# DVE's 32x32 block transposes for softmax sums, the spreading of their reciprocals and the maxima, in place of TensorE products

## The chip, the cores and the metric

The kernel runs on one core of a Trainium2 chip. The metric is device time in microseconds of one execution; 0.2% of it (2.6 us) is about what can be told from no change. Engines are named as the profile does: PE (TensorE; PEld its weight loads), DVE (VectorE), ACT (ScalarE), POOL (GpSimd), SP (the queue that issues nearly all DMAs).

## The reference

Two independent layers over 2048 positions and 448 channels, concatenated. Half A is an S4D convolution: a kernel `K` made of exponentials of 256 modes per channel, an FFT convolution with `u`, and a skip term. Half B is multi-head attention with 16 heads of width 28; the part that matters here:

```python
scores = jnp.einsum("bhqd,bhkd->bhqk", q, k) * scale
p = _softmax(scores, axis=-1)
o = jnp.einsum("bhqk,bhkd->bhqd", p, v)
return (lambda x, *d: x.transpose(*d))(o, 0, 2, 1, 3).reshape(B, S, D) @ wo
```

## The kernel before

All work is recorded through a wrapper (`Kept`, line 77), so nearly every instruction has line 77 in the profile and is told by its tiles. In a first part (about 225 us: projections of q, k, v and the start of half A) a scheduler is free to order each engine's instructions (`KEPT["p"]` is empty). From `nc.kept = KEPT["a"]` on, every engine runs in the order in which the code calls it.

**The main loop** has 256 steps (line 1061 on): 16 units (4 head groups of 4 heads times 4 blocks of 512 queries), 16 steps each, one step per 128 keys. `ORDER` (line 35) is a step's order: four score products `s0` to `s3` (tile `pss`, then an exponential on ACT into `p`), four products `m0` to `m3` for the row maxima of the unit that comes next (tile `pm`; `m0` is followed by a Relu on ACT into `rl`, `m1` by a fused add-and-maximum on DVE, custom instruction `rl<-pm,rl`; `m2` and `m3` by a DVE reduction `mx<-pm`), `pv` (the product with v of the step before, tile `po`), two places `f` for a piece of half A or of the output projection (`slot`, line 1012), and three places `v` for one DVE instruction of half A's powers (`g`, `zg`). POOL computes other powers (`e`, `eu`) all the while. The maxima run 19 steps ahead of their use (`sm = s + NK + LEAD`).

All `pm` tiles (maxima, pieces, and the products described next) take turns in a ring of three PSUM buffers (`w_tile`, line 127): a product waits until the third tile before it has been read.

**At a unit's end** (`fin`, line 789) ACT copies the finished `po` to SBUF as `o`: for each head 28 rows of output, and in row 28 of its 32 the softmax sum, because v carries a column of ones. Then, as pieces that take a place `f` each two and four places later (`UG`, `soon_slot`):
- `sums`: PE products `sel,o` pick the sums, queries on partitions; DVE takes their reciprocals `r` from PSUM; ACT spreads each over 32 columns into `rb`.
- `scale`: PE products `ident,rb` turn `rb` back into the layout of `o`; DVE multiplies `on = o * pm`, the second operand in PSUM. `on` goes to DRAM or, in the last head group, to four output projections `project` (products `ua,og` and `ua,on`).

**At the end of a unit's maxima** `max_join` (line 210) joins three maxima per row (`m`, 128x16), and two places later `max_end` (line 214) has PE transpose `m` to 16x128 in PSUM (`ident,m`), from which DVE makes minus the maximum as a high and a low part (`mh`, two instructions from PSUM); two DMAs put them into two rows of `qhat`, so that the score product subtracts the maximum. The score products of that unit begin three steps after the join.

The other PE pieces: `e,g` and `w,ko` (56 blocks of half A's kernel, done at about step 198), `ua,w` and `ua,mt` (transform of u, 64 pieces, to about step 101), `yk,mw`, `p,mw` and `zi,wb` (spectrum and inverse transform, from step 192 on).

Of the kernel before, what the change touches and what calls it, by code (L numbers as in the profile page):

```python
# [8 lines left out]
F32 = mybir.dt.float32  # L9
# [83 lines left out]
def body(ctx, tc, a, out):  # L93
# [26 lines left out]
    sel = const.tile([128, HG], F32, name="sel")  # L120
    kones = const.tile([128, 1], F32, name="kones")
    w1 = const.tile([128, 2, 128], F32, name="w1")

# [87 lines left out]
        m_u[u, 1] = q_p.tile([128, HG * 4], F32, name="m1", bufs=2)  # L211
        nc.vector.tensor_reduce(m_u[u, 1], m_u[u].rearrange("p a b c -> p (a b) c")[:, :, :n], axis=AX.X, op=ALU.max)

    def max_end(u, ps):
        nc.tensor.transpose(ps[:16, :128], m_u[u, 1], ident)
        mh = q_p.tile([16, 2, 128], F32R, name="mh")
        nc.vector.tensor_scalar(mh[:, 0, :], ps[:16, :128], -1.0, None, op0=ALU.mult)
        nc.vector.scalar_tensor_tensor(mh[:, 1, :], ps[:16, :128], -1.0, mh[:, 0, :].bitcast(F32),
                                       op0=ALU.mult, op1=ALU.subtract)
        mh_u[u] = mh  # L220

    def max_put(u, queue=nc.sync):
        for i in range(2):
            queue.dma_start(q_u[u][4 * (DH + i):4 * (DH + i) + 1, :, :].rearrange("p h (t q) -> p (h t) q", t=4).bitcast(F32),
                                mh_u[u][:, i, :].bitcast(F32))


    with ExitStack() as st:
        sst, xst, wst = ExitStack(), ExitStack(), ExitStack()
# [91 lines left out]
        nc.sync.dma_start(sel, a["sel"])  # L321
        nc.sync.dma_start(w1, a["w1"])
        def split_w(s):
            for k in range(NCK):
# [276 lines left out]
        nc.scalar.activation(half_pi[:1], half_pi[:1], AF.Exp)  # L601
        n_st.close()
        max_join(0, 2)
        max_end(0, ps_t.tile([128, CQ], F32, name="pt"))
        max_put(0, nc.scalar)
        sst.close()


# [180 lines left out]
    def fin(u, s_):  # L789
        g, c = divmod(u, NQ)  # L790
        o = kq_p.tile([128, CQ], F32, name="o")
        nc.scalar.activation(o, o_u[u], AF.Copy)
        on = kq_p.tile([128, CQ], F32, name="on", bufs=2)
        rb = kq_p.tile([128, 4, HG, 32], F32, name="rb")
        og = og_u.pop(u, None)

        def sums():
            pw = w_tile()
            for t in range(4):
                mm32(pw[:, t * HG:(t + 1) * HG], o[:, t * 128:(t + 1) * 128], sel, start=True, stop=True)  # L800
            r = kq_p.tile([128, 4, HG], F32, name="r", bufs=2)
            nc.vector.reciprocal(r, pw[:, :4 * HG].rearrange("p (t h) -> p t h", h=HG))
            nc.scalar.activation(rb, r[:, :, :, None].to_broadcast([128, 4, HG, 32]), AF.Copy)

        def scale():
            pw = w_tile()
            for t in range(4):
                mm32(pw[:, t * 128:(t + 1) * 128], rb[:, t].rearrange("p h e -> p (h e)"), ident, True, True)
            nc.vector.tensor_tensor(on, o, pw, ALU.mult)
            if g < G - 1:  # L810
                nc.sync.dma_start(on_d[c][g], on)
            else:
# [12 lines left out]

        soon_slot(UG[1], sums)
        soon_slot(UG[2], scale)

    fk = {}

# [94 lines left out]
    k_seeds(0)  # L925
    k_seeds(0)

    urgent, back = collections.deque(), collections.deque()
# [82 lines left out]

    def slot(s_):
        n_slot[0] += 1
        if urgent and urgent[0][0] <= n_slot[0]:
            urgent.popleft()[2]()
        elif s_ >= NS and f_slot(s_, "s"):
            pass
        elif p_due and p_due[0][0] <= s_:
            p_due.popleft()[1]()
        elif m_due and m_due[0][0] <= s_:  # L1020
            m_due.popleft()[1]()
        elif u_due and u_due[0][0] <= s_:
            u_part(*u_due.popleft()[1:])
        else:
            f_slot(s_, "s") or f_slot(s_, "f")
# [35 lines left out]
    for s in range(NS):  # L1061
# [59 lines left out]
    s = NS  # L1121
    while urgent or p_due or m_due or u_due or any(q[k] for q in (f_jobs, f_tasks, f_loaded) for k in "sf"):
        slot(s)
        s += 0.5
    assert not k_due and not powers["g"] and not powers["e"]
# [4 lines left out]
def constants():  # L1130
    import numpy as np
    k = {}
    k["ident"] = np.eye(128)
    sel, ones = np.zeros((128, HG)), np.zeros((128, 1))
    for j in range(HG):
        sel[32 * j + DH, j] = 1.0
        ones[32 * j + DH:32 * j + DH + 2] = 1.0
    k["sel"], k["kones"] = sel, ones
# [46 lines left out]
```

## Time and profile before

| | us |
|---|---|
| median of 3 runs (lowest, highest) | 1278.05 (1277.69, 1278.42) |
| the profiled execution | 1278.83 |
| its span in the profile | 1277.0 |
| busy: PE, ACT, DVE, POOL | 1216.2, 967.0, 922.6, 843.6 |
| first step's first exponential (unit 0) | 231.2 |

Some 1.8 us lie outside the span. The page gives busy time per engine; the windows give it for a stretch; the timeline lists instructions in time with the idle time before them and what ended it. Matmuls are pipelined, so a matmul's duration overlaps the next one's: what a product costs PE is read from start to start.

### The profile page before, as it was taken

Reading aid. Unit: us, or ns where it says so; the run is one execution under the profiler, and the core shown is the slowest. Engines: PE = TensorE matmul, PEld = TensorE weight load, DVE = VectorE, ACT = ScalarE, POOL = GpSimd, SP = SyncE. Lnnn points to the kernel's source line nnn. Section 1 sums busy time; section 2 is a strip of 40 time slices with the busy share of each in tenths; the row PEclk is TensorE's granted clock in tenths of the full one; section 3 lists DMA queues with packets and bytes.
Section 4 is the critical chain, followed back from the end, with each engine's and each line's share of the span. In section 5 each row is a group of like instructions: output and inputs, shape, how many; then the busy total and the mean of one; then the engine's idle time right before and its main releaser. Section 6 shows DMA issues by size and latency. Waiting matters only on the chain.

```text
span 1277.0 us, 33251 instructions
## 1 busy us (share of the span) xinstructions
PE 1216.2 (95%) x12593; PEld 692.5 (54%) x12593; DVE 922.6 (72%) x2106; ACT 967.0 (76%) x2162; POOL 843.6 (66%) x728
## 2 busy tenths in 40 slices
PE   6788888999999999999999999999999999999998
PEld 4666764555555555555555555555555555544433
DVE  5788966877777877778778988888887645645111
ACT  5888865788888888888888888888887656656552
POOL 2666740798788888878689999989995222324321
PEclk9999898899999999999999999999999999999999
DMA  6678789436554645475533133432224533657656
GB/s 194 211 258 290 275 278 359 124 88 187 159 154 114 169 118 159 123 224 177 171 101 96 57 80 105 145 91 71 83 60 149 171 139 135 205 162 237 203 163 174
DMA packets 203528, 206.22 MB, mean 161 GB/s; under 512 B 98344, under 2 KB 162408, under 8 KB 201320
## 3 DMA queue, kind: packets, MB, share of 16 engines
q1 hardware_dynamic: 202840, 203.50, 51.8%
q8 instruction: 99, 1.62, 0.5%
q10 hardware_dynamic: 528, 0.59, 0.2%
q14 instruction: 61, 0.50, 0.1%
HBM read 121.60 MB, written 82.18 MB: 160 GB/s over the span
## 4 chain that ended last, share of the span: by engine, by line
PE 79%; DVE 9%; ACT 5%; issue 3%; POOL 2%; DMA 1%; SPq 1%; ACTq 0%; POOLq 0%; DVEq 0%
PE pm L77 44%; PE pss L77 17%; PE po L77 17%; DVE tri L77 1%; ACT tri L77 1%; DVE mx L77 1%; DVE sg L77 1%; SPq L77 1%; ACT rl L77 1%; DVE hl L77 1%; DVE px L77 1%; ACT p L77 1%; PE pt L77 1%; POOL p L77 1%; DVE g L77 1%
## 5 line engine op out<-in xcount | busy, mean ns | idle before, releaser
L77 ACT ACTIVATE p<-pss 128x512 f32<-128x512 f32 x1024 | 561.3, 611 | 111.5 <-PE pss L77 108.4
L77 PE MATMUL pss<-qhat,khat 128*128 128x512 f32 x1024 | 402.8, 399 | 1.5 <-ACT p L77 1.4
L77 DVE TENSOR_REDUCE mx<-pm 128x1 f32<-128x512 f32 x480 | 308.3, 683 | 108.9 <-PE pm L77 106.8
L77 PE MATMUL pm<-khat,qhat 128*128 128x512 f32 x749 | 326.3, 439 | 6.6 <-ACT rl L77 4.4
L77 POOL TENSOR_TENSOR e<-e,sdb 128x256 f32<-128x256 f32 x168 | 201.8, 1201 | 111.4 <-ACT e L77 62.2
L77 PE MATMUL po<-p,v 128*32 128x512 f32 x2048 | 269.1, 594 | 0.0
L77 POOL TENSOR_TENSOR e<-e,eu 128x256 f32<-128x256 f32 x168 | 248.1, 1477 | 13.2
L77 PEld LDWEIGHTS pm<-khat,qhat 128*128 128x128 f32 x749 | 141.2, 189 | 202.8 <-ACT p L77 46.9
L77 DVE CUSTOM_DVE_ANT_0 rl<-pm,rl 128x512 f32<-128x512 f32 x259 | 178.2, 688 | 73.7 <-ACT rl L77 70.8
L77 PEld LDWEIGHTS pss<-qhat,khat 128*128 128x128 f32 x1024 | 190.4, 188 | 46.1 <-issue 10.8
L77 POOL TENSOR_TENSOR eu<-e,sdb 128x256 f32<-128x256 f32 x168 | 201.9, 1202 | 0.0
L77 POOL TENSOR_TENSOR p<-pr,pr 64x448 f32<-64x448 f32 x64 | 73.1, 1142 | 161.4 <-PE pm L77 134.7
L77 ACT ACTIVATE rl<-pm 128x512 f32<-128x512 f32 x259 | 156.8, 607 | 15.4 <-PE pm L77 9.4
L77 DVE TENSOR_TENSOR g<-g,zg 128x128 f32<-128x128 f32 x392 | 161.9, 413 | 3.4
L77 PE MATMUL pm<-kdif,qhat 128*128 128x512 f32 x249 | 100.9, 405 | 6.0 <-DVE xn L77 4.1
L77 PE MATMUL pm<-xh,khat 128*128 128x512 f32 x256 | 85.0, 423 | 12.1 <-DVE hl L77 5.3
L77 DVE TENSOR_TENSOR zg<-g,zg 128x128 f32<-128x128 f32 x224 | 88.0, 393 | 5.0
L77 PEld LDWEIGHTS pm<-e,g 128*32 128x32 f32 x3584 | 57.2, 109 | 43.9 <-issue 16.2
L77 DVE TENSOR_TENSOR pr<-pm,ub 128x448 f32<-128x448 f32 x64 | 37.0, 619 | 56.4 <-PE pm L77 42.0
L77 PE MATMUL pm<-e,g 128*32 128x64 f32 x3584 | 73.0, 222 | 1.9 <-POOL e L77 1.3
L77 ACT ACTIVATE y<-pm 128x448 f32<-128x448 f32 x48 | 26.5, 553 | 58.2 <-PE pm L77 35.9
L77 ACT ACTIVATE ub<-pm 128x224 f32<-128x224 f32 (+1 forms) x96 | 38.7, 448 | 39.5 <-PE pm L77 37.4
(135 smaller groups left out, 1436.7 us busy)
## 6 DMA issues: line engine op xcount, KB each, us to landing
sdb<-sd SPq DMA_DIRECT2D x55, 336.0 KB
qhat<-q SPq DMA_DIRECT2D x64, 256.0 KB
khat<-k SPq DMA_DIRECT2D x64, 256.0 KB
sd<-sg SPq DMA_DIRECT2D x8, 1456.0 KB
k<-hl SPq DMA_DIRECT2D x16, 512.0 KB
mw<-in_mw SPq DMA_DIRECT2D x16, 512.0 KB
sd<-qhat SPq DMA_DIRECT2D x8, 896.0 KB
yu_d<-ub SPq DMA_DIRECT2D x64, 112.0 KB
```

What stands on the lines that cost most here:

```text
L77: i = f(*args, **kw)
```

## The change

It touches three places, and the bookkeeping that goes with them. A DVE "turn" here is one STREAM_TRANSPOSE that transposes each 32x32 block of a tile by itself.

1. **Sums** (in `fin`): DVE turns `o` (128x512) into an SBUF tile `rb`, so that queries stand on partitions and each block's column 28 holds a head's sums; the reciprocal reads these 16 columns from SBUF. No product, no `pm` tile.
2. **Spread and scale**: ACT spreads `r` as before, into a second use of the same `rb` buffer; DVE turns it into `on`; then `on = o * on`, both operands in SBUF.
3. **Maxima**: DVE makes the high and low parts directly from `m` (128x16 each, side by side in one 128x32 SBUF tile `mh`), turns them (`mt`), and four DMAs instead of two put 32-column pieces into the two rows of `qhat`. This is called at once behind `max_join`, at the end of the step, not two places later. The first unit (before the loop) keeps the old way, as `max_first`.

The three steps of a unit's end are no longer pieces that take a place `f`: a new queue `free` runs them one place after another, ahead of the piece that the place gives out. So per unit three places become free for other pieces. The constant `sel` and its DMA are gone.

```diff
-    def max_end(u, ps):
-        nc.tensor.transpose(ps[:16, :128], m_u[u, 1], ident)
-        mh = q_p.tile([16, 2, 128], F32R, name="mh")
-        nc.vector.tensor_scalar(mh[:, 0, :], ps[:16, :128], -1.0, None, op0=ALU.mult)
-        nc.vector.scalar_tensor_tensor(mh[:, 1, :], ps[:16, :128], -1.0, mh[:, 0, :].bitcast(F32),
-                                       op0=ALU.mult, op1=ALU.subtract)
-        mh_u[u] = mh
+    def max_end(u):
+        m = m_u[u, 1]
+        hl = q_p.tile([128, 2, HG * 4], F32R, name="mh")
+        nc.vector.tensor_scalar(hl[:, 0], m, -1.0, None, op0=ALU.mult)
+        nc.vector.scalar_tensor_tensor(hl[:, 1], m, -1.0, hl[:, 0].bitcast(F32), op0=ALU.mult, op1=ALU.subtract)
+        mh_u[u] = q_p.tile([128, 32], F32, name="mt")
+        nc.vector.transpose(mh_u[u], hl.bitcast(F32).rearrange("p i n -> p (i n)"))
+
+    def max_put(u):
+        row = q_u[u][4 * DH:4 * DH + 8:4].bitcast(F32).rearrange("p h (t b q) -> p (h t) b q", t=4, b=4)
+        for b in range(4):
+            nc.sync.dma_start(row[:, :, b, :], mh_u[u][32 * b:32 * b + 32, :])
...
-        rb = kq_p.tile([128, 4, HG, 32], F32, name="rb")
         og = og_u.pop(u, None)
+        t_ = {}
+        turned = lambda: kq_p.tile([128, NK, 32], F32, name="rb")
+        flat = lambda t: t.rearrange("p b e -> p (b e)")
 
         def sums():
-            pw = w_tile()
-            for t in range(4):
-                mm32(pw[:, t * HG:(t + 1) * HG], o[:, t * 128:(t + 1) * 128], sel, start=True, stop=True)
-            r = kq_p.tile([128, 4, HG], F32, name="r", bufs=2)
-            nc.vector.reciprocal(r, pw[:, :4 * HG].rearrange("p (t h) -> p t h", h=HG))
-            nc.scalar.activation(rb, r[:, :, :, None].to_broadcast([128, 4, HG, 32]), AF.Copy)
+            t = turned()
+            nc.vector.transpose(flat(t), o)
+            t_["r"] = kq_p.tile([128, NK], F32, name="r", bufs=2)
+            nc.vector.reciprocal(t_["r"], t[:, :, DH])
+
+        def spread():
+            t = turned()
+            nc.scalar.activation(t, t_["r"][:, :, None].to_broadcast([128, NK, 32]), AF.Copy)
+            nc.vector.transpose(on, flat(t))
 
         def scale():
-            pw = w_tile()
-            for t in range(4):
-                mm32(pw[:, t * 128:(t + 1) * 128], rb[:, t].rearrange("p h e -> p (h e)"), ident, True, True)
-            nc.vector.tensor_tensor(on, o, pw, ALU.mult)
+            nc.vector.tensor_tensor(on, o, on, ALU.mult)
...
-        soon_slot(UG[1], sums)
-        soon_slot(UG[2], scale)
+        for i, f in enumerate((sums, spread, scale)):
+            free.append((n_slot[0] + 1 + i, f))
...
     def slot(s_):
         n_slot[0] += 1
+        while free and free[0][0] <= n_slot[0]:
+            free.popleft()[1]()
         if urgent and urgent[0][0] <= n_slot[0]:
             urgent.popleft()[2]()
...
         if sm < NS and sm % NK == NK - 1:
-            def end(un=sm // NK):
-                max_end(un, w_tile())
-                max_put(un)
             max_join(sm // NK)
-            soon_slot(UG[0], end)
+            max_end(sm // NK)
+            max_put(sm // NK)
```

**Where the instructions stand.** First, DVE's queue around the end of unit 0. Before, from the reduction of `m2` in the step in which the unit ends (`ISA rl,mx` is the fused maximum, `ISA mx` reads its accumulator):

```order
L77 TENSOR_REDUCE mx<-pm_3343 128x1
L77 TENSOR_TENSOR g<-g,zg 128x16x16
L77 ISA rl,mx<-pm_3364,rl 128x512
L77 ISA mx 128x1
L77 TENSOR_TENSOR zg<-g,zg 128x256
L77 RECIPROCAL r<-pm_3372 128x16
L77 TENSOR_TENSOR g<-g,zg 128x16x16
L77 TENSOR_REDUCE mx<-pm_3414 128x1
L77 TENSOR_REDUCE mx<-pm_3421 128x1
L77 ISA rl,mx<-pm_3441,rl 128x512
L77 ISA mx 128x1
L77 TENSOR_TENSOR on<-o,pm_3448 128x512
```

The same place in the changed kernel, from the power `g` just ahead of the unit's end:

```order
L77 TENSOR_TENSOR g<-g,zg 128x32x16
L77 STREAM_TRANSPOSE rb<-o 128x512
L77 RECIPROCAL r<-rb 128x16
L77 TENSOR_TENSOR zg<-g,zg 128x256
L77 TENSOR_REDUCE mx<-pm_3339 128x1
L77 TENSOR_REDUCE mx<-pm_3346 128x1
L77 TENSOR_TENSOR g<-g,zg 128x16x16
L77 ISA rl,mx<-pm_3367,rl 128x512
L77 ISA mx 128x1
L77 TENSOR_TENSOR zg<-g,zg 128x256
L77 STREAM_TRANSPOSE on<-rb 128x512
L77 TENSOR_TENSOR on<-o,on 128x512
```

The turn of `o` and the reciprocal now stand ahead of the two reductions of the very step in which the unit ends; the turn into `on` and the multiplication stand together ahead of the reductions of the step behind it.

Second, DVE's queue at the end of a unit's maxima (unit 1's). Before:

```order
L77 TENSOR_REDUCE m_3096<-mx 128x16
L77 ISA rl,mx<-pm_3107,rl 128x512
L77 ISA mx 128x1
L77 TENSOR_TENSOR g<-g,zg 128x32x16
L77 TENSOR_SCALAR mh<-pm_3131 16x128
L77 SCALAR_TENSOR_TENSOR mh<-pm_3131,mh 16x128
L77 TENSOR_TENSOR zg<-g,zg 128x256
L77 TENSOR_REDUCE mx<-pm_3145 128x1
```

In the changed kernel:

```order
L77 TENSOR_REDUCE m_3094<-mx 128x16
L77 TENSOR_SCALAR mh<-m_3094 128x16
L77 SCALAR_TENSOR_TENSOR mh<-m_3094,mh 128x16
L77 STREAM_TRANSPOSE mt<-mh 128x32
L77 ISA rl,mx<-pm_3114,rl 128x512
L77 ISA mx 128x1
L77 TENSOR_TENSOR g<-g,zg 128x32x16
L77 TENSOR_TENSOR zg<-g,zg 128x256
L77 TENSOR_REDUCE mx<-pm_3145 128x1
```

The two `mh` instructions and the turn now follow the join at once, each needing the one before it, and the next step's fused maximum stands behind them.

Third, PE's queue behind the end of unit 0, from the place `f` in which `sums` stood. Before:

```order
L77 MATMUL pm_3372<-sel,o 32x4 x16
L77 MATMUL po<-p,v 32x512 x4
L77 MATMUL pm_3397<-w_111,ko 32x128 x8
L77 MATMUL pm_3414<-khat,qhat 128x512
```

In the changed kernel, the same place:

```order
L77 MATMUL pm_3378<-w_110,ko 32x128 x8
L77 MATMUL po<-p,v 32x512 x4
L77 MATMUL pm_3397<-ua,w_110 32x448 x4
L77 MATMUL pm_3417<-khat,qhat 128x512
L77 MATMUL pss<-qhat,khat 128x512
```

The products with `sel` and `ident` are gone, and pieces of half A have moved up into their places.

In the first part, too, the scheduler's order of some instructions differs on PE, DVE, ACT and SP, although only `sel`'s DMA has gone from it.

More of the change, by code (lines that the diff above doesn't have):

```diff
@@ L119, in body @@
     nc.sync.dma_start(ident, a["ident"])
-    sel = const.tile([128, HG], F32, name="sel")
     kones = const.tile([128, 1], F32, name="kones")
@@ L212, in max_join, with max_first @@
         nc.vector.tensor_reduce(m_u[u, 1], m_u[u].rearrange("p a b c -> p (a b) c")[:, :, :n], axis=AX.X, op=ALU.max)
-    def max_end(u, ps):
-        nc.tensor.transpose(ps[:16, :128], m_u[u, 1], ident)
-        mh = q_p.tile([16, 2, 128], F32R, name="mh")
+    def max_end(u):
[9 more added lines that the diff above has]
+            nc.sync.dma_start(row[:, :, b, :], mh_u[u][32 * b:32 * b + 32, :])
+    def max_first(ps):
+        nc.tensor.transpose(ps[:16, :128], m_u[0, 1], ident)
+        mh = q_p.tile([16, 2, 128], F32R, name="m0")
         nc.vector.tensor_scalar(mh[:, 0, :], ps[:16, :128], -1.0, None, op0=ALU.mult)
@@ L219, in max_end @@
                                        op0=ALU.mult, op1=ALU.subtract)
-        mh_u[u] = mh
-    def max_put(u, queue=nc.sync):
         for i in range(2):
-            queue.dma_start(q_u[u][4 * (DH + i):4 * (DH + i) + 1, :, :].rearrange("p h (t q) -> p (h t) q", t=4).bitcast(F32),
-                                mh_u[u][:, i, :].bitcast(F32))
+            nc.scalar.dma_start(q_u[0][4 * (DH + i):4 * (DH + i) + 1, :, :].rearrange("p h (t q) -> p (h t) q", t=4)
+                                .bitcast(F32), mh[:, i, :].bitcast(F32))
     with ExitStack() as st:
@@ L320, in body @@
         nc.sync.dma_start(kones, a["kones"])
-        nc.sync.dma_start(sel, a["sel"])
         nc.sync.dma_start(w1, a["w1"])
@@ L603, in body @@
         max_join(0, 2)
-        max_end(0, ps_t.tile([128, CQ], F32, name="pt"))
-        max_put(0, nc.scalar)
+        max_first(ps_t.tile([128, CQ], F32, name="pt"))
         sst.close()
@@ L926, in body @@
     k_seeds(0)
-    urgent, back = collections.deque(), collections.deque()
+    urgent, free = collections.deque(), collections.deque()
     powers = {"g": collections.deque(), "e": collections.deque()}
@@ L1121, in body @@
     s = NS
-    while urgent or p_due or m_due or u_due or any(q[k] for q in (f_jobs, f_tasks, f_loaded) for k in "sf"):
+    while urgent or free or p_due or m_due or u_due or any(q[k] for q in (f_jobs, f_tasks, f_loaded) for k in "sf"):
         slot(s)
@@ L1133, in constants @@
     k["ident"] = np.eye(128)
-    sel, ones = np.zeros((128, HG)), np.zeros((128, 1))
+    ones = np.zeros((128, 1))
     for j in range(HG):
-        sel[32 * j + DH, j] = 1.0
         ones[32 * j + DH:32 * j + DH + 2] = 1.0
-    k["sel"], k["kones"] = sel, ones
+    k["kones"] = ones
     k["pw2"] = np.tile(2.0 ** np.arange(LV), (128, 1))
```

## The prediction

> **What bounds the kernel now.** I read the page's chain first, then the windows, then the timeline at three places. The chain that ended last:
>
> ```profile
> PE 79%; DVE 9%; ACT 5%; issue 3%; POOL 2%; DMA 1%; SPq 1%; ACTq 0%; POOLq 0%; DVEq 0%
> ```
>
> PE carries it. The windows (after the stretch and its length: PE, PEld, DVE, ACT, POOL busy in us) tell the stages apart:
>
> ```profile
> 0.00:225.00 225.00, 179.69 (x742) 135.41 (x742) 170.06 (x358) 164.03 (x387) 108.11 (x150) 0.91 0.79 267
> 720.00:800.00 80.00, 79.57 (x984) 45.89 (x981) 70.11 (x169) 67.32 (x152) 76.97 (x62) 1.00 0.29 84
> 1040.00:1120.00 80.00, 79.96 (x769) 41.42 (x769) 44.64 (x91) 51.81 (x101) 25.00 (x21) 1.00 0.44 144
> ```
>
> In the loop PE is full. But at 720 to 800 us DVE is busy for 70.1 of 80 us (88%) and POOL for 77.0 (96%); only in the last quarter have they room (44.6 and 25.0). An undisturbed step of unit 8, first PE, then DVE:
>
> ```profile
> 756.18 0.50 PE L77 MATMUL pm<-khat,qhat 128*128 128x512 f32 x1
> ...
> 757.69 0.40 PE L77 MATMUL pm<-khat,qhat 128*128 128x512 f32 x1
> ...
> 759.70 0.50 PE L77 MATMUL pm<-khat,qhat 128*128 128x512 f32 x1
> ```
>
> ```profile
> 756.41 0.43 DVE L77 TENSOR_TENSOR zg<-g,zg 128x256 f32<-128x256 f32 x1
> 756.75 1.28 DVE L77 TENSOR_REDUCE mx<-pm 128x1 f32<-128x512 f32 x2
> 757.95 0.41 DVE L77 TENSOR_TENSOR g<-g,zg 128x256 f32<-128x256 f32 x1
> 758.62 0.69 DVE L77 CUSTOM_DVE_ANT_0 rl<-pm,rl 128x512 f32<-128x512 f32 x1 [0.26 <-ACT rl L77]
> ```
>
> A step is 759.70 − 756.18 = 3.52 us. DVE reduces `m2` 0.57 us after its product starts; the product `m1` of the next step, three tiles on in the ring, needs that tile back and starts 1.51 after `m2`. DVE may thus be some 0.2 us late before PE stands still: what DVE gets in front of these reductions beyond that, PE pays, and PE is the bound. This decides the case.
>
> **What goes.** A unit's end before (PE, ACT and DVE, each by itself):
>
> ```profile
> 734.00 0.50 PE L77 MATMUL pm<-khat,qhat 128*128 128x512 f32 x1
> ...
> 735.50 0.39 PE L77 MATMUL pm<-khat,qhat 128*128 128x512 f32 x1
> ...
> 736.05 0.43 PE L77 MATMUL pm<-sel,o 128*32 128x4 f32 x32
> ...
> 740.17 1.08 PE L77 MATMUL pm<-ident,rb 128*32 128x128 f32 x32
> 741.06 1.04 PE L77 MATMUL po<-p,v 128*32 128x512 f32 x8
> ...
> 742.48 0.50 PE L77 MATMUL pm<-khat,qhat 128*128 128x512 f32 x1
> ```
>
> ```profile
> 734.16 0.60 ACT L77 ACTIVATE o<-po 128x512 f32<-128x512 f32 x1 [0.15 <-PE po L77]
> ```
>
> ```profile
> 734.61 1.28 DVE L77 TENSOR_REDUCE mx<-pm 128x1 f32<-128x512 f32 x2
> ...
> 737.50 0.25 DVE L77 RECIPROCAL r<-pm 128x16 f32<-128x16 f32 x1
> ...
> 741.32 0.69 DVE L77 TENSOR_TENSOR on<-o,pm 128x512 f32<-128x512 f32 x1
> ```
>
> From `m2` at 734.00 to the one two steps on at 742.48 are 8.48 us, 1.44 over two clean steps; `ident,rb` alone takes 741.06 − 740.17 = 0.89. The end of a unit's maxima (unit 10's):
>
> ```profile
> 837.64 0.48 PE L77 MATMUL pm<-khat,qhat 128*128 128x512 f32 x1
> ...
> 839.50 0.50 PE L77 MATMUL pm<-khat,qhat 128*128 128x512 f32 x1 [0.20 <-DVE mx L77]
> ...
> 841.63 0.50 PE L77 MATMUL pm<-khat,qhat 128*128 128x512 f32 x1
> ```
>
> ```profile
> 836.27 0.19 DVE L77 TENSOR_REDUCE m<-mx 128x16 f32<-128x48 f32 x1
> 836.56 0.69 DVE L77 CUSTOM_DVE_ANT_0 rl<-pm,rl 128x512 f32<-128x512 f32 x1
> ...
> 837.93 0.28 DVE L77 TENSOR_SCALAR mh<-pm 16x128 fp32r<-16x128 f32 x1 [0.33 <-PE pm L77]
> ```
>
> That step takes 3.99, 0.47 over a clean one. Twelve units lie in the loaded part (to about 960 us): 12 x (1.44 + 0.47) = **22.9 us go**. In the last quarter, three more ends at about 1.2 (0.28 for `sel,o`, 0.89 for `ident,rb`) and three maxima at 0.3: **4.5**. The tail:
>
> ```profile
> 1254.40 0.60 ACT L77 ACTIVATE o<-po 128x512 f32<-128x512 f32 x1 [1.14 <-PE po L77]
> ...
> 1257.76 0.69 DVE L77 TENSOR_TENSOR on<-o,pm 128x512 f32<-128x512 f32 x1 [1.41 <-PE pm L77]
> ```
>
> Today `on` is ready 4.05 after `o` starts. The new chain, o 0.6, turn 0.68, reciprocal 0.25, spread 0.63, turn 0.68, multiplication 0.69, with some 0.3 between them, is as long (3.8). But PE loses 1.2 of products there, and by the order four of eight last pieces `zi,wb` (about 0.4 each) move ahead into steps where ACT sets the pace: I take **3** (0 if they only move, 4 at most).
>
> **What a turn costs.** No row shows one. One-pass DVE instructions over 512 columns take 0.69 (the two above) or 0.64 (half of 1.28); half as long if it moved two elements at a time, about 1.3 if four-byte data took two passes. I take 0.68, between ends of 0.34 and 1.3, since all 512-column rows lie there. The Trainium skill, "VectorE: DVE Perf Modes", "The three transpose paths", has 311 ns for 128x128 in bf16; with its 0.96 GHz clock, my estimate for 512 columns is 0.71, which would add 0.7 us to the sum.
>
> **What the turns put in DVE's queue at a unit's end.** Replayed on the rows above. `o` is done at 734.76, so the first turn runs 734.82 to 735.50, the reciprocal to 735.78, `zg` (0.43) to 736.2; only then the reductions, at 736.25 for 734.61. The product `m1` follows its reduction's start by 0.73 (838.77 to 839.50 at the maxima), so at 736.98 for 735.50. The next piece needs the second reduction too (737.53), so the step is 5.05 for 3.52. In the next step DVE runs without a gap: `g` 0.41, fused maximum 0.69, `zg` 0.42, turn 0.68, multiplication 0.69, power 0.38; the reduction starts at 740.87, `m1` at 741.6 for 740.55, and the step is 4.6. Then DVE has caught up. Together 2.65 over two clean steps. Where the order puts a piece `ua` (0.75 us on PE) between the product with v and `m2`, that much of a step's stall is hidden: both steps in two of the twelve ends (0.8 + 0.35), one in three; seven have none.
>
> **POOL stands in the way as well.** Before, loop instructions of DVE that run beside POOL have an operand in PSUM. `on = o * on`, and the two `mh` instructions, no longer do. In the first part there are such instructions (DVE's, then POOL's, then all DVE instructions of two groups with least, median and longest ns):
>
> ```profile
> 69.67 1.43 DVE L77 TENSOR_SCALAR tri<-tri 128x1232 f32<-128x1232 f32 x1
> ...
> 71.32 1.95 DVE L77 TENSOR_TENSOR tri<-tri 128x1232 f32<-128x1232 f32 x1
> ```
>
> ```profile
> 69.42 1.02 POOL L77 TENSOR_TENSOR x_e<-qhat 128x336 f32<-128x336 f32 x1
> 70.52 1.46 POOL L77 TENSOR_TENSOR qhat<-qhat,x_e 128x336 f32<-128x336 f32 x1
> ```
>
> ```profile
> L77 DVE TENSOR_TENSOR tri<-pn,pw x8: 1419/1426/1441, 23.6 to 157.9; 128x1232 f32<-128x1232 f32 x8
> L77 DVE TENSOR_SCALAR tri<-tri x8: 782/796/1627, 27.2 to 160.4; 128x1232 f32<-128x1232 f32 x8
> ```
>
> With a PSUM operand the time never varies (1419 to 1441). From SBUF alone it ranges from 782 to 1627: the one at 69.67 ends 0.66 after POOL's instruction at 69.42 does, as if it had begun only then; POOL's next gets in, and the DVE instruction at 71.32 ends 1.3 after that one. In the loop POOL's instructions are long:
>
> ```profile
> L77 POOL TENSOR_TENSOR e<-e,eu 128x1024 f32<-128x1024 f32 x56 | 133.6, 2386 | 4.4
> L77 POOL TENSOR_TENSOR eu<-e,sdb 128x256 f32<-128x256 f32 x56 | 35.4, 632 | 0.0
> ```
>
> They last 0.63 to 2.39; a DVE instruction that arrives at random waits about 0.7 (at least 0, at most 2.4). For the multiplication I take 0.7. The two `mh` can wait twice, 0.5 and then a whole one (some 1.25), if both are held; I take 1.0 for both, between 0 and 1.75. The Trainium skill states such a rule: "SBUF — State Buffer", "SBUF: two separate sides", has DVE instructions with two SBUF inputs, or in a two-port mode, and POOL's exclude each other for a whole instruction. The trace agrees for these rows; by the rule the turns would be held only in a two-port mode, which no row here can show.
>
> **The sum.** Unit ends: seven at 2.65 + 0.7, two at 1.15 + 0.7, three at 1.9 + 0.7 = 23.5 + 3.7 + 7.8 = **35.0**. Maxima: the three small instructions (about 0.2 each; 0.19 and 0.28 above) stand ahead of the fused maximum, which delays the reductions to 838.67, a stall of 0.4 (much as now); with POOL's 1.0, nine at 1.4 and three, behind a piece, at 0.6: **14.4**. In all 49.4 − 22.9 − 4.5 − 3 = +19.0: 1278.8 + 19.0 = 1297.8 for an execution like the profiled one, which is 0.8 above the median of the runs shown: **1297**. Two more DMA issues per unit stand on SP, some 0.6 each, three steps (10.5 us) ahead of their reader: nothing. The first part's reshuffled order I put at 0, ±3: PE stands idle for 45 of its 225 us, so nothing there is tight on one engine alone.
>
> **Rivals.**
> - *Queue alone, no wait for POOL*: 7 x 2.65 + 2 x 1.15 + 3 x 1.9 + 9 x 0.4 = 30.2 against 30.4: 1278, no change (1271 to 1285 with the turn's and the tail's bounds). Against it speak the 782 to 1627; for it, that POOL's long instructions differ from those. Chance 0.20.
> - *PE's gain is all that counts* (the other side): DVE takes the turns into its idle tenth and the ring holds: 1278 − 30 = 1248, or up to 1271 with half the stalls. It decides if `m1` starts within some 0.3 us of its place. For it: 16 x 2 turns are only 22 us, DVE has 10 of 80 us free. Against: the free time lies behind the reductions, not before them. Chance 0.13.
> - *Turns dearer*, by two passes (0.6 x 2 x 12 = 14.4) or held by POOL (0.7 x 2 x 12 = 16.8): 1312 to 1314, range to 1325. Chance 0.15.
> - *The change does not do what it says*: the four DMAs land after the unit's first score products; each unit then waits. Over 6 us of landing would be needed, and then slower still. Chance 0.04.
>
> **How the numbers follow.** The forecast (1286 to 1311, from POOL's bounds) has 0.48. 0.2% is 2.6 us, about what can be told. Faster: 0.13 and a third of the first rival, 0.20; no change 0.08; slower 0.72. The range leaves out the faster rival's far half and the dearest end: 1271 to 1316.
>
> **What would show it.** STREAM_TRANSPOSE near 0.68; `on<-o,on` with a median near 1.4 and a spread as wide as POOL's instructions, but 0.68 in the last quarter; PE waiting for `mx` in the two steps behind each unit's end (about 5.0 and 5.3 us in units 7 to 11), less where a piece `ua` precedes; units 7 to 11 near 59 to 60 us, now 57; the last quarter some 7 us shorter. Wrong it would be if `m1` there started at its place, or if DVE's new instructions never varied.

## The result, and the profile after

The changed kernel takes 1325.01 us (median of four runs, 1320.09 to 1328.8), the kernel before 1278.18 beside it: **1.0365 times as long (95% interval 1.0328 to 1.0401)**, 47 us slower. Forecast were 1297, at most 1316. The profiled execution of the changed kernel is its fastest, 1320.09 us with a span of 1318.3 against 1277.0: the traces account for 41.3 us; of the 5 us between that execution and the median there is no trace.

Where the 41.3 us are, from the starts of each unit's first exponential in the two traces (changed kernel minus before): first part **+7.4**, units 0 to 11 **+24.0**, unit 12 **+11.5**, units 13 to 15 **+2.8**, after the last exponential **-4.4**. The end of a unit falls into the time of the next one, so units 0 to 11 hold eleven unit ends, and twelve ends of maxima. In these units PE has the same other pieces as before (4824 products), and 704 products with `sel` and `ident,rb` and 12 transposes less; they take 24.0 us longer all the same.

First the new instructions, all of them in one row each (count, then least, median and longest ns, then first and last start):

```profile
L77 DVE STREAM_TRANSPOSE rb<-o x16: 711/712/714, 301.5 to 1300.7; 128x512 f32<-128x512 f32 x16
L77 DVE STREAM_TRANSPOSE on<-rb x16: 703/712/715, 305.3 to 1302.4; 128x512 f32<-128x512 f32 x16
L77 DVE TENSOR_TENSOR on<-o,on x16: 671/1151/2134, 306.1 to 1303.1; 128x512 f32<-128x512 f32 x16
...
L77 DVE TENSOR_SCALAR mh<-m x15: 174/176/1647, 287.1 to 1214.3; 128x16 fp32r<-128x16 f32 x15
L77 DVE SCALAR_TENSOR_TENSOR mh<-m,mh x15: 174/486/2270, 287.3 to 1214.8; 128x16 fp32r<-128x16 f32 x15
```

A turn of 128x512 takes 0.71 us and never varies, though 14 of the 32 began while an instruction of POOL was running. The multiplication and the two `mh` vary by factors of 3 to 13. Behind the end of unit 7 one sees why, and what it does (DVE, POOL, PE of the changed kernel; in brackets the idle time before an instruction and what ended it):

```profile
757.84 0.71 DVE L77 STREAM_TRANSPOSE on<-rb 128x512 f32<-128x512 f32 x1
758.59 1.82 DVE L77 TENSOR_TENSOR on<-o,on 128x512 f32<-128x512 f32 x1
760.34 0.41 DVE L77 TENSOR_TENSOR g<-g,zg 128x256 f32<-128x256 f32 x1
760.67 1.28 DVE L77 TENSOR_REDUCE mx<-pm 128x1 f32<-128x512 f32 x2
```

```profile
758.56 1.30 POOL L77 TENSOR_TENSOR e<-e,eu 128x512 f32<-128x512 f32 x1
```

```profile
761.40 0.50 PE L77 MATMUL pm<-khat,qhat 128*128 128x512 f32 x1 [1.72 <-DVE mx L77]
```

POOL's instruction starts 0.03 before the multiplication and ends at 759.86; the multiplication ends 0.55 later, as if it had begun only near then. It is so throughout: each of the 12 multiplications of over 0.8 us ends 0.55 behind the end of a POOL instruction that overlapped its start, and each of the 12 `mh` of over 0.4 us ends 0.03 behind one. The reductions, queued behind it, start at 760.67 and PE's product at 761.40, after 1.72 us of waiting. Over the loaded part (225 to 960 us) PE's waits for `mx` grew so (first before, then changed; us in total, times, longest; PEld rows are waits of a weight load, part of which lies beneath PE's work):

```profile
PEld pm L77 <- DVE mx L77: 49.0, 133, 0.8
...
PE pm L77 <- DVE mx L77: 1.9, 10, 0.2
```

```profile
PEld pm L77 <- DVE mx L77: 90.4, 154, 3.2
...
PE pm L77 <- DVE mx L77: 31.0, 32, 2.8
```

So far this is the prediction's picture. Two things are not in it. The first is one step of 13.2 us in unit 12. POOL and PE there, changed kernel:

```profile
1010.07 4.77 POOL L77 TENSOR_TENSOR p<-pr,pr 64x448 f32<-64x448 f32 x4 [13.81 <-DVE pr L77]
1014.91 1.91 POOL L77 TENSOR_TENSOR e<-e,sdb 128x1024 f32<-128x1024 f32 x1
1016.78 1.91 POOL L77 TENSOR_TENSOR eu<-e,sdb 128x1024 f32<-128x1024 f32 x1
1018.76 2.32 POOL L77 TENSOR_TENSOR e<-e,eu 128x1024 f32<-128x1024 f32 x1
```

```profile
1021.13 1.08 PE L77 MATMUL pm<-e,g 128*32 128x64 f32 x32 [6.45 <-POOL e L77]
```

and POOL before:

```profile
968.83 2.40 POOL L77 TENSOR_TENSOR e<-e,eu 128x1024 f32<-128x1024 f32 x1
980.11 4.80 POOL L77 TENSOR_TENSOR p<-pr,pr 64x448 f32<-64x448 f32 x4 [8.88 <-PE pm L77]
```

`p<-pr,pr` are POOL's four products of a piece of the spectrum, the first of half A's later stages. Before, they stood behind the last power `e`. Now the piece has got a place `f` that the sums no longer take, and its four products stand in POOL's queue ahead of the last three powers of a block: POOL is idle for 13.81 us until DVE's `pr` comes, then works 4.77 at `p`, and only then at the powers, for whose last PE waits 6.45 us with everything behind it. From 1019.5 on the granted clock is then halved for 6.83 us (more on this behind runs 3 and 4). The second is the first part. Windows at two of its places (length; PE, PEld, DVE, ACT, POOL busy; granted clock; DMA share; GB/s), before and changed:

```profile
40.00:60.00 20.00, 17.02 (x81) 13.43 (x81) 16.46 (x30) 17.20 (x42) 12.57 (x15) 1.00 0.54 185
...
140.00:180.00 40.00, 36.99 (x156) 30.37 (x156) 31.29 (x58) 32.65 (x81) 23.85 (x33) 0.89 0.76 248
```

```profile
40.00:60.00 20.00, 20.00 (x87) 16.55 (x85) 13.96 (x29) 15.97 (x42) 11.48 (x12) 0.83 0.39 129
...
140.00:180.00 40.00, 29.36 (x125) 23.84 (x123) 31.13 (x58) 31.01 (x81) 23.54 (x28) 0.87 0.65 214
```

From 40 to 60 us PE is busy for 3.0 us more than before and the DMA engines for less; but there the granted clock is 0.83 for 1.00, and PE runs only six instructions more. From 140 to 180 us, at nearly the same clock, PE runs 31 instructions less and is busy for 7.6 us less. The same work stands in another order, and the loop starts 7.4 us later.

### The profile page after: what moved, and what is told of

The parts are those of the page before. It is cut to its first block, busy times and chain, and to the rows that moved or that the text cites. A ratio compares the mean times of both kernels' runs of the same rounds, so it can differ in the third digit from the quotient of the medians.

```text
span 1318.3 us, 31241 instructions
## 1 busy us (share of the span) xinstructions
PE 1211.1 (92%) x11554; PEld 677.5 (51%) x11554; DVE 963.7 (73%) x2153; ACT 970.5 (74%) x2162; POOL 846.1 (64%) x728
## 5 line engine op out<-in xcount | busy, mean ns | idle before, releaser
L77 PE MATMUL pm<-khat,qhat 128*128 128x512 f32 x749 | 330.6, 445 | 38.4 <-DVE mx L77 33.0
L77 POOL TENSOR_TENSOR e<-e,eu 128x256 f32<-128x256 f32 x168 | 249.5, 1485 | 13.2
L77 PE MATMUL pm<-xh,khat 128*128 128x512 f32 x256 | 86.4, 431 | 17.3 <-DVE kb L77 9.2
L77 ACT ACTIVATE y<-pm 128x448 f32<-128x448 f32 x48 | 26.5, 553 | 62.0 <-PE pm L77 43.7
L77 PEld LDWEIGHTS po<-p,v 128*32 128x32 f32 x2048 | 54.8, 110 | 26.7 <-issue 21.5
L77 DVE TENSOR_TENSOR pr<-pm,ub 128x448 f32<-128x448 f32 x64 | 36.7, 615 | 43.4 <-PE pm L77 22.9
```

The lines of the kernel that those rows point to most:

```text
L77: i = f(*args, **kw)
```

## The experiments

All runs stand beside runs of the kernel before (medians 1277.9 to 1278.4). The times are medians. The table gives, from each profiled execution, what differs from the kernel before in each stage (us; stages by the unit's first exponential, as above), so that each edit can be read where it acts.

| kernel | time | ratio (95%) | first part | units 0-11 | unit 12 | 13-15 | tail |
|---|---|---|---|---|---|---|---|
| changed kernel | 1325.0 | 1.0365 (1.0328-1.0401) | +7.4 | +24.0 | +11.5 | +2.8 | -4.4 |
| 1 sel loaded | 1312.5 | 1.0267 (1.0250-1.0284) | -2.1 | +27.2 | +11.5 | +2.7 | -4.5 |
| 2 spectrum held | 1297.5 | 1.0152 (1.0137-1.0167) | -0.8 | +25.1 | +0.6 | -1.3 | -4.5 |
| 3 sums alone | 1302.8 | 1.0192 (1.0177-1.0207) | -2.8 | +19.9 | +9.5 | -1.4 | -2.8 |
| 4 maxima alone | 1290.7 | 1.0096 (1.0081-1.0111) | -0.8 | +12.4 | +0.9 | +1.0 | +0.2 |
| 5 multiplication from PSUM | 1290.9 | 1.0101 (1.0086-1.0116) | -0.9 | +17.7 | +0.3 | -0.4 | -4.5 |
| 6 maxima from PSUM | 1296.5 | 1.0142 (1.0125-1.0159) | -1.5 | +24.0 | +0.7 | +0.4 | -4.5 |
| 7 late places | 1295.2 | 1.0130 (1.0115-1.0145) | -0.8 | +17.3 | +2.3 | +2.5 | -4.5 |
| 8 before, dead turns | 1292.4 | 1.0110 (1.0095-1.0125) | -0.7 | +12.7 | +1.2 | +0.1 | +0.3 |
| 9 before, sel late | 1288.6 | 1.0083 (1.0067-1.0099) | +8.6 | +0.1 | 0.0 | +0.9 | 0.0 |
| 10 last units only | 1272.9 | 0.9961 (0.9948-0.9974) | -0.9 | +0.2 | -0.6 | -2.1 | -2.5 |
| 11 behind | 1275.6 | 0.9980 (0.9971-0.9989) | -1.3 | +4.6 | 0.0 | -1.4 | -3.3 |
| 12 behind, locked | 1274.6 | 0.9973 (0.9963-0.9983) | -2.1 | +1.8 | -0.8 | -2.1 | -2.7 |

**1. One DMA put back.**

```
 const: + sel = const.tile([128, HG], F32, name="sel")
 after the DMA of kones: + nc.sync.dma_start(sel, a["sel"])
```

> The changed kernel with one thing put back: the 128x4 table sel is still loaded by SP in the first part (nothing reads it). By the order, the first part is then that of the kernel before, row for row, and only the loop has the turns. Theory A (the first part's 7.4 us in the profile after come from the order that this one DMA fixes): about 7 us below the changed kernel's 1325, 1315 to 1320, with the first exponential at about 231 us instead of 238.6. Rival (the 7.4 us are the lower clock of that execution, or its spread): 1322 to 1328, first exponential near 238.

1312.5, 12.5 us less; the first exponential of this kernel, and of the changed one (first start in each row):

```profile
L77 ACT ACTIVATE p<-pss x1024: 578/602/729, 229.1 to 1292.1; 128x512 f32<-128x512 f32 x171
```

```profile
L77 ACT ACTIVATE p<-pss x1024: 578/602/732, 238.6 to 1298.3; 128x512 f32<-128x512 f32 x171
```

The first part is 9.5 us shorter with a table that nothing reads, and the time is even below theory A's 1315 to 1320. (The spans differ by 6.4 only: the changed kernel's profiled execution was its fastest, and unit 1 takes 69.1 us here for 65.7. There an `mh` that began 0.01 us ahead of POOL's power in the changed kernel, and lasted 0.17, begins 0.01 behind it and lasts 2.37, and PE waits 2.06 for 0.27.) Theory A stands for the changed kernel; run 9 turns it round.

**9. The same DMA taken out of the first part of the kernel before.**

```
-        nc.sync.dma_start(sel, a["sel"])       (first part)
     nc.kept = KEPT["a"]
+    nc.sync.dma_start(sel, a["sel"])
```

> The kernel before, with one DMA moved: SP loads sel where the loop begins, not in the first part. No turn is in it. By the order its first part is then that of the changed kernel, row for row, on every engine. Theory A (the first part's loss comes from the order that this one DMA decides): 1285 to 1290, the first exponential at 237 to 240 us instead of 231. Rival (the turns, or the chance of an execution, made the first part longer): 1278 to 1280.

1288.6: the kernel before, with no turn in it, loses 10.3 us. Its windows and its first exponential:

```profile
40.00:60.00 20.00, 19.30 (x89) 15.65 (x87) 14.74 (x29) 17.50 (x44) 11.49 (x12) 0.94 0.40 134
...
140.00:180.00 40.00, 29.79 (x122) 24.18 (x121) 30.21 (x56) 30.28 (x78) 23.63 (x28) 0.83 0.63 209
```

```profile
L77 ACT ACTIVATE p<-pss x1024: 572/605/715, 239.8 to 1262.3; 128x512 f32<-128x512 f32 x171
```

They are near the changed kernel's. Up to the first exponential PE, ACT, POOL and DVE run the changed kernel's instructions in the changed kernel's order here, and those of the kernel before in run 1. The twelve profiled executions with the old order have their first exponential at 228.4 to 231.2 us, the two with the new at 238.6 and 239.8. The granted clock isn't the reason: over the first 225 us it is 0.91 on average in this run and in the kernel before. What costs 9 us there is the order that the scheduler finds when this DMA isn't in its list. Which of the moved instructions is the late one wasn't tried and stays open.

**2. The spectrum held back** (with sel loaded):

```
-        if n_slot[0] < f_next[kind] + gap:
+        if n_slot[0] < f_next[kind] + gap or kind == "s" and powers["e"]:
```

> As the run with sel loaded, and a piece of the spectrum is given no place while powers e of a block are still to be issued; POOL's order is then that of the kernel before, row for row. Theory B (the 13.2 us step of unit 12 is POOL's queue: four products of the spectrum piece p<-pr,pr stand ahead of the last three powers e, which PE needs): another 9 to 12 us less than with sel alone, about 1306 where that gives 1317; no step of unit 12 over 8 us. Rival (that step is DVE's turns or the lock between DVE and POOL): within 3 us of the run with sel alone.

1297.5, 15.0 us less; unit 12 goes from +11.5 to +0.6, units 13 to 15 from +2.7 to -1.3, and the longest step of unit 12 from 13.2 to 4.9 us. Theory B stands, with more than the 9 to 12 us that it gave. The turns are all in this kernel: its time is what the change costs without its two side effects.

**3 and 4. The two halves alone** (sel loaded; the other half as in the kernel before, in both functions and places).

> The turns for the sums and for the spreading alone; the maxima go through PE as in the kernel before; sel is loaded, so the first part is as before. Theory C (queue at the unit's end plus POOL's lock on the multiplication, the prediction's terms): 35.0 stalls - 17.3 - 3.5 - 3 = +11, and the spectrum piece's 11.5 in unit 12, which the sums' freed places cause: about 1300 (1296 to 1305). Rival (queue alone, without a lock): 26.6 - 23.8 + 11.5 = +14 at most, +3 without the piece: 1281 to 1292.

> The turn for the maxima alone, the sums and the spreading through PE as in the kernel before; POOL's order is as before, row for row. Theory C (lock of POOL on the two mh): 14.4 - 5.6 - 0.9 = +8, 1286 (1282 to 1290). Rival (queue alone): 3.6 - 6.5 = -3, 1275.

1302.8 and 1290.7. Unit 12's loss belongs to the sums (+9.5 against +0.9), as their freed places should have it. In units 0 to 11 the sums cost 19.9 and the maxima 12.4, both above the terms with the lock (17.7 and 8.8) and far above those without. Together they cost 25.1 and not 32.3. How the maxima cost it is seen before unit 11 (DVE, POOL, PE of run 4):

```profile
900.81 2.30 DVE L77 SCALAR_TENSOR_TENSOR mh<-m,mh 128x16 fp32r<-128x16 f32 x1
```

```profile
900.72 2.36 POOL L77 TENSOR_TENSOR e<-e,eu 128x1024 f32<-128x1024 f32 x1
```

```profile
904.02 0.50 PE L77 MATMUL pm<-khat,qhat 128*128 128x512 f32 x1 [2.00 <-DVE mx L77]
```

An instruction of 0.17 us of work lasts 2.30, from just behind the start to just behind the end of POOL's power, and PE waits 2.00. Two us later the granted clock is halved (a window as above, and PE's product with v in it):

```profile
906.00:909.40 3.40, 3.40 (x27) 1.51 (x27) 1.92 (x5) 1.60 (x4) 3.24 (x4) 0.50 0.24 61
```

```profile
906.92 1.93 PE L77 MATMUL po<-p,v 128*32 128x512 f32 x8
```

These eight products take 1.93 us here and 1.04 at the full clock. No theory had this, and it bears on all the sizes in the table. From the first to the last exponential the kernel before never loses clock, nor do runs 8, 9, 10 and 12. In units 0 to 11 the clock is halved for 3.41 us twice in the changed kernel and in run 5, three times in runs 1, 2, 4 and 6, four times in run 3, five in run 7 and once in run 11. Of all 32 such stretches of the loop, 31 begin during a PE wait of 1.48 us or more, or within 2.1 us of its end; several such waits have none behind them, so when the clock falls isn't explained. With PE full a stretch costs at most 3.41 x 0.5 = 1.7 us, my estimate: up to 6.8 of run 3's 19.9, 5.1 of run 4's 12.4, but also 5.1 only of run 2's 25.1. That would be nearly all of the 7.2 by which the halves together cost less than their sum. No run sets the clock apart.

**5 and 6. The lock taken away by an operand in PSUM** (both on run 2):

```
 5:  -            nc.vector.transpose(on, flat(t))
     +            t_["pw"] = w_tile()
     +            nc.vector.transpose(t_["pw"], flat(t))
     -            nc.vector.tensor_tensor(on, o, on, ALU.mult)
     +            nc.vector.tensor_tensor(on, o, t_["pw"], ALU.mult)
 6:  -        m_u[u, 1] = q_p.tile([128, HG * 4], F32, name="m1", bufs=2)
     +        m_u[u, 1] = w_tile()[:, :HG * 4] if u else q_p.tile(...)
```

> The run with the spectrum held back (1297.5), with one operand changed: the second turn writes a tile of the ring pm in PSUM, and the multiplication reads it there (on = o * pm). No engine's order changes. Theory C (the multiplication waits for POOL because both its operands are in SBUF): its mean falls from 1.49 us to 0.68 and it never varies, which frees 9 us on DVE in eleven units; 5 to 9 us less, 1289 to 1293. Rival 1 (the lock hides, the queue alone costs): within 2 us of 1297.5. Rival 2 (the ring's tile, held from the turn to the multiplication, delays PE's next product more than the lock did): 1300 or more.

> The run with the spectrum held back (1297.5), with the joined maxima m written into a ring tile in PSUM, so that both instructions that make mh have a PSUM operand. No engine's order changes. Theory C: their means fall from 0.44 and 0.79 us to about 0.25 each, 8 us less on DVE in eleven units: 1289 to 1293. Rival (queue alone): within 2 us of 1297.5.

Run 5: 1290.9, 6.6 less. Its multiplication, and PE's new waits in the loaded part:

```profile
L77 DVE TENSOR_TENSOR on<-o,pm x16: 671/686/689, 297.9 to 1274.1; 128x512 f32<-128x512 f32 x16
```

```profile
PEld pm L77 <- DVE on L77: 13.2, 11, 1.5
...
PE pm L77 <- DVE on L77: 7.0, 11, 0.9
```

Run 6: 1296.5, 1.0 us less, though there too the variation is gone:

```profile
L77 DVE TENSOR_SCALAR mh<-pm x15: 174/175/176, 278.3 to 1194.3; 128x16 fp32r<-128x16 f32 x15
L77 DVE SCALAR_TENSOR_TENSOR mh<-pm,mh x15: 174/174/175, 278.5 to 1194.5; 128x16 fp32r<-128x16 f32 x15
```

That POOL holds these instructions is shown by both: with one operand in PSUM none of 46 ever waits. That the waits themselves cost time is shown for the multiplication at its place only (and one stretch at half the clock, up to 1.7 of run 5's 7.4 us in units 0 to 11, went with them). A ring tile isn't free either: PE now waits for `on` in run 5, which it did not do in run 2 to speak of, and run 6 lost in some units what it won in others. Theory C's 4 to 8 us for the maxima failed. Why their waits cost so little here stays open.

**8. Two turns that nothing reads, in the kernel before.**

```
+        if u < 12:
+            for i in range(2):
+                free.append((n_slot[0] + 1 + i, lambda: nc.vector.transpose(
+                    kq_p.tile([128, CQ], F32, name="dead"), o)))
```

> The kernel before, unchanged in all it computes, with two more turns of o on DVE in each of the first twelve units' ends (their result is not read), one in each of the two slots behind the unit's end. No other engine's order changes. The price of two turns in that queue by itself, without POOL's lock (if turns are not held). Theory of the queue: 0.7 to 1.5 us a unit, 1287 to 1296; turns of 0.71 throughout. Rival (DVE takes them into its idle tenth): 1278 to 1280. If turns are held by POOL, their longest is over 1.5 us.

1292.4. The turns, and PE's waits:

```profile
L77 DVE STREAM_TRANSPOSE dead<-o x24: 703/710/715, 293.4 to 978.3; 128x512 f32<-128x512 f32 x24
```

```profile
PEld pm L77 <- DVE mx L77: 58.7, 139, 1.5
...
PE pm L77 <- DVE mx L77: 7.6, 17, 1.0
```

No turn is held by POOL, though 15 of the 24 began while one of its instructions was running, so the rival of dearer turns is out. Two turns of 0.71 in front of the reductions cost 12.7 us in units 0 to 11, 1.15 for each of the eleven unit ends in them, though PE still has its own products there to cover them, and the clock is full. Of 17.0 us of turns DVE's idle time takes in some 3.

**7. Other places for the turns** (on run 2): in units 0 to 11 they take a place `v` when no power `g` is left for it.

```
         if powers["g"]:
             powers["g"].popleft()()
+        elif free:
+            free.popleft()[1]()
...
+            free.append((n_slot[0] + (30 if u < 12 else 1) + i, f))
```

> The run with the spectrum held back (1297.5), and in the first twelve units the first turn, the second turn and the multiplication stand in places of DVE's queue where the filter's powers g leave none, most of them behind the two reductions instead of ahead of them. PE's and POOL's orders do not change. Theory D (the price is where in the queue the turns stand: work behind the reductions falls into DVE's idle time): the sums' stalls of about 20 over the removed work fall by 12 to 18, 1280 to 1286. Rival (the price is DVE's work and POOL's lock as a whole, wherever they stand): 1293 to 1298.

1295.2, 2.3 less: theory D missed, but so did the edit. The free places `v` come in a row, so the first turn mostly came to stand behind the reductions, but in ten of the twelve units the second turn and the multiplication stand together ahead of the next ones (DVE and PE, unit 11):

```profile
930.25 0.71 DVE L77 STREAM_TRANSPOSE on<-rb 128x512 f32<-128x512 f32 x1 [0.62 <-ACT rb L77]
931.00 2.21 DVE L77 TENSOR_TENSOR on<-o,on 128x512 f32<-128x512 f32 x1
933.13 1.28 DVE L77 TENSOR_REDUCE mx<-pm 128x1 f32<-128x512 f32 x2
```

```profile
933.86 0.50 PE L77 MATMUL pm<-khat,qhat 128*128 128x512 f32 x1 [2.39 <-DVE mx L77]
```

The stall moved to another step and stayed. The run says little on places behind the reductions; run 11 was made for that.

**11 and 12. One piece a step, behind the reductions** (sums by turns, maxima through PE, sel loaded, spectrum held).

```
 11: def sums():   turn of o into t
     def scale():  r = w_tile()[:, :NK]
                   nc.vector.reciprocal(r, t[:, :, DH])
                   nc.vector.tensor_tensor(t, t, r[:, :, None].to_broadcast([128, NK, 32]), ALU.mult)
     def back():   turn of t into on, and its DMA
     at the end of each step:  if later: later.popleft()()     (units 0 to 11)
 12: -            r = w_tile()[:, :NK]
     +            w_tile()
     +            r = kq_p.tile([128, NK], F32, name="r", bufs=2)
```

> The sums by turns in all units, maxima through PE, sel loaded, spectrum held back; in the twelve loaded units the three pieces stand one in each step, behind the two reductions at its end, and none has two operands in SBUF: turn; reciprocal into a ring tile in PSUM and multiplication of the turned o by it, spread as it is read; turn back. ACT's spreading goes. Theory D (price by place and lock): DVE has 0.44 us free in a step and the three pieces have 0.71, 0.94 and 0.71, so about 1 us of stall a unit, 12 x (1.0 - 1.44) - 5 at the end: 1267 to 1273. Rival (DVE's work ahead of the next step's fused maximum costs what it did ahead of the reductions, 2.8 a unit): 12 x 1.4 - 5: 1288 to 1292.

> The run with the pieces behind the reductions (1275.6), with the reciprocals in SBUF instead of the ring tile in PSUM, so that the multiplication of the turned o has both operands in SBUF again; a ring tile is still counted off, and no engine's order changes. It parts place from lock. Theory C (POOL holds a multiplication of two SBUF operands, and the step has no room for it wherever it stands): the multiplication's mean rises from 0.69 to 1.3 to 1.6 us, and the time by 6 to 10, as the lock cost at the unit's end: 1282 to 1286. Rival (behind the reductions the wait falls into idle time, so place alone is what counts): within 2 us of 1275.6.

1275.6 and 1274.6, 0.2 and 0.3% faster than before, with intervals that leave out 1. Multiplication and PE's waits in the loaded part, run 11 and then run 12:

```profile
L77 DVE TENSOR_TENSOR rb<-rb,pm x16: 686/687/690, 298.1 to 1258.0; 128x512 f32<-128x512 f32 x16
```

```profile
PEld pm L77 <- DVE mx L77: 62.6, 156, 1.1
...
PE pm L77 <- DVE mx L77: 5.9, 20, 0.7
...
PE pm L77 <- DVE rb L77: 5.6, 9, 1.1
```

```profile
L77 DVE TENSOR_TENSOR rb<-rb,r x16: 691/1028/2876, 297.2 to 1253.0; 128x512 f32<-128x512 f32 x16
```

```profile
PEld pm L77 <- DVE mx L77: 71.7, 167, 2.4
...
PE pm L77 <- DVE mx L77: 9.9, 25, 1.6
```

Theory D stands in run 11 against its rival: the sums cost 4.6 in units 0 to 11 for 19.9 in run 3. Its own term was too hopeful even so: 12 x (1.0 - 1.44) = -5.3 for these units. PE runs 704 products less there, some 11 x 1.44 = 16 us by the prediction's price, and the units still take 1.8 to 4.6 longer. In the loaded units, then, even the best place found makes the turns about as dear as the products that they replace. Run 12 refutes theory C at this place. POOL holds the multiplication again, up to 2.88 us, but the time doesn't rise: behind the reductions the wait seems to fall into time that DVE had free, and PE waits for the ring tile `rb` of run 11 (5.6 us) are gone; how the two share isn't shown. The two runs' intervals overlap. Between runs 3 and 12 lie 18 us in units 0 to 11; place, the spacing of one piece a step and the missing spreading on ACT were changed together and are not parted, and up to 6.8 of the 18 are run 3's four stretches at half the clock.

**10. The turns where DVE has room**: units 12 to 15 as in the changed kernel, sums of units 0 to 11 and all maxima as before, sel loaded, spectrum held.

```
+        if u < 12:
+            soon_slot(UG[1], sums_pe)
+            soon_slot(UG[2], scale_pe)
+            return
         for i, f in enumerate((sums, spread, scale)):
```

> The turns only where DVE has room: units 12 to 15 have their sums, spreading and multiplication by turns as in the changed kernel; the units before, and all maxima, go through PE as in the kernel before; sel is loaded in the first part, and the spectrum is held back while powers e are left. Theory (the loop's loss is the loaded twelve units' alone, and the end gains): 1278 - 4.5 at the tail - 0 to 1 in the last quarter = 1272 to 1275. Rival (the tail's gain came from pieces moved ahead in the loop, and goes without them): 1277 to 1279.

1272.9, 0.9961 of the kernel before (0.9948 to 0.9974): the lowest median of all, though run 12's interval overlaps. In the loaded part PE waits for `mx` as it did before (48.7 us for 49.0), and the end gains 5.2:

```profile
PEld pm L77 <- DVE mx L77: 48.7, 130, 0.8
```

## Why the prediction was wrong, point by point

- **The turns' queue: right.** The two steps behind a unit's end were forecast at 5.05 and 5.3 in units 7 to 11, 10.35 together. In the changed kernel they take 11.30, 10.24, 9.60, 10.26 and 9.40 there, mean 10.2 (by the exponentials' starts); in the first a stretch at half the clock has its part. Units 7 to 11 take 60.4 us on average for the forecast 59 to 60. Turns took 0.71, the estimate named beside the 0.68 that the sum used, and were not held. (5.05 and 4.6 are 2.61 over two clean steps, not 2.65, which changes the sum by 0.3.)
- **POOL's lock: right in kind, near in size at the unit's end.** 12 x 0.7 = 8.4 were forecast; taking it away gave 7.4 in units 0 to 11 (run 5 against 2), net of what the ring tile costs and with one stretch at half the clock less. The median of the multiplication is 1.15 for "near 1.4", 0.67 to 0.69 in the last units as forecast, but for one of 1.70. The Trainium skill's rule, "SBUF — State Buffer", "SBUF: two separate sides", agrees with the instructions of two SBUF inputs (671 to 2134 ns) and with the turn and the reciprocal, which have one input and never waited. The TENSOR_SCALAR has one input too and did wait (174 to 1647); by the Trainium skill's rule it would have to be in a two-port mode. The prediction's rows of `tri` fit that, with 782 ns for a TENSOR_SCALAR from SBUF and 1419 for the TENSOR_TENSOR with a PSUM operand over the same 1232 columns; for 128x16 no row shows it. What such a wait costs in time hangs on its place (run 12).
- **The maxima: the size stays open.** 14.4 - 5.6 = 8.8 were forecast; alone they cost 12.4, of which up to 5.1 is the clock, and beside the sums 5.2 (25.1 - 19.9). The wait for POOL was seen rightly, but without it the cost hardly fell (run 6).
- **Units 0 to 11 together: near, and in part by luck.** 49.4 - 22.9 = +26.5 forecast, +24.0 measured. But the forecast has no term for the clock, which falls behind the very waits that it priced: up to 3.4 of the 24.0, and 5.1 of run 2's 25.1. Without these the terms would be up to 6 us too high. The tail: -3 forecast, -4.4 measured; the last unit's `on` starts 3.07 us behind `o` (3.36 before), so most of it is pieces that left the tail.

```profile
1300.06 0.60 ACT L77 ACTIVATE o<-po 128x512 f32<-128x512 f32 x1 [1.14 <-PE po L77]
```

```profile
1303.13 0.69 DVE L77 TENSOR_TENSOR on<-o,on 128x512 f32<-128x512 f32 x1
```

- **"The first part's reshuffled order I put at 0, ±3: PE stands idle for 45 of its 225 us, so nothing there is tight on one engine alone": this step failed.** Measured +7.4 in the profile, 10.3 in run 9 by the one DMA alone. An engine's idle time over 225 us doesn't show that its order is free to change: in the new order PE runs 31 instructions less from 140 to 180 us, and the loop starts later in both kernels that have it. The two orders were there to be compared, but no row told which of them was the better, and ±3 was a guess.
- **"In the last quarter, three more ends ... and three maxima at 0.3: 4.5": this step failed, and by its sign.** The profile has +14.3 in units 12 to 15. It counted what PE no longer does and did not follow what moves into the freed places. A spectrum piece did, and of its instructions those on POOL passed the powers; run 2 gives 15.0 us for that. Without it units 12 to 15 still yield only 0.7, with the tail 5.2 for the 7.5 forecast: four of the tail's pieces `zi,wb` have moved into them, at the prediction's 0.4 each some 1.6 us that the term of 4.5 leaves out.

Run 2, the change without these two, is at 1297.5, the forecast's number: 25.1 - 0.7 - 4.5 - 0.8 = 19.1 for 26.5 - 4.5 - 3 = 19.0. Part of that is luck, since the last quarter's miss made up for the units' and the tail's. Of the rivals, the queue alone (1278) and PE's gain alone (1248 to 1271) are out by runs 2, 5 and 8, dearer turns by run 8. So is the rival of DMAs that land too late: the last of the four is issued 7 to 10 us ahead of its unit's first exponential, and no wait of PE in the loop is put down to a DMA.

## What to carry to other kernels

When work leaves an engine, ask first what takes its place: follow every instruction of each piece that moves up, on each queue that it passes, since a piece that waits in an in-order queue holds all that stands behind it. Price an instruction by what stands behind it in its queue: net of the products that they replace, the sums' turns and the lock cost 20 us ahead of the reductions that PE waits for, and 2 to 5 when they stood one a step behind them. Look at the granted clock wherever a new wait appears: a wait can cost more than its own length. Compare the order of parts that the change doesn't touch as well, above all where a scheduler is free, and when they differ, run the old kernel in the new order before explaining anything else.

## What the runs showed of the hardware that was not expected

- POOL holds a DVE instruction of 0.17 us for up to 2.27, by the size of POOL's instruction and not of its own; a 32x32 turn of the same memory beside it never varies (703 to 715 ns over 128x512 f32, 211 to 214 over 128x32).
- The reciprocal (253 to 256 ns from SBUF) isn't held, although 7 of 16 began while an instruction of POOL was running; the equally small TENSOR_SCALAR is.
- In the loop the granted clock falls to half for 3.41 us at or behind PE waits of 1.48 to 2.81 us in eight of the traces, though not behind each such wait, and for 6.83 us at a wait of 6.45.
